# A late 4 MB zero fill sent as 120 rows on fifteen DMA engines and 8 rows on eight

## The chip, the cores and the metric

One core of a Trainium2 chip. The metric is the device time of one execution in microseconds (us). The four runs of the kernel before lie within 0.2% of each other (802.07 to 803.28); all runs compared here are of the fast state, except four kernels that ran once each and whose state is therefore unknown (marked "state unknown" below). Times in the profile count from the start of the span, that is from the first to the last instruction. The span of the kernel before is 802.6 us, its median time 802.9 us.

## The reference

A decoding step of attention over the last 4096 of 32768 cached positions, a gated feed-forward layer, and the gradients of all of it. What matters here is the gradient of the two caches: they have the caches' full shape, and outside the window they are zero.

```
"k_cache": (1, 8, 32768, 256)  bf16        # so is v_cache
W = min(4096, max(256, Sk // 4))           # 4096
k = jnp.repeat(k_cache[:, :, Sk - W:, :], rep, axis=1)
v = jnp.repeat(v_cache[:, :, Sk - W:, :], rep, axis=1)
...
_out, _vjp = jax.vjp(_f, A_x, A_k_cache, A_v_cache, ...)
_grads = _vjp(grad_out)
```

So 2 x 8 x 28672 x 256 zeros in bf16, 235 MB, have to be written, beside some 100 MB of loads and other results.

## The kernel before

SBUF is the core's on-chip memory; the fills read it as 128 partitions (rows, `p=128` below). Zeros lie in the arena in SBUF and are sent to the two outputs (`out_2`, `out_3`) in fills, large DMAs that write nothing but zeros. Most are issued on GpSimd's queue (`ZQ`), one after another until 700 us. The last ones, the late jobs, go out on SyncE's queue (`LD`), mixed with the last real results.

```
ZW = 8192
LD = nc.sync
ZQ = nc.gpsimd
... # cut
def zero_rows(o, g, n0, n1, f):
    reg = o[0, g, 0:Sk - W, :].rearrange("s d -> (s d)")[n0 * 128 * ZW:n1 * 128 * ZW]
    return reg.rearrange("(n p f) -> n p f", p=128, f=f)

late_jobs = [(out_2, G - 1, 5, 7, 2 * ZW), (out_3, G - 1, 0, 6, 2 * ZW), (out_3, G - 1, 6, 7, ZW)]
... # cut: everything else
            if it == 6:
                nc.vector.memset(ar(ZW, ZW), 0.0)

        for o, g, n0, n1, f in late_jobs:
            reg = zero_rows(o, g, n0, n1, f)
            for i in range(reg.shape[0]):
                LD.dma_start(out=reg[i], in_=ar(2 * ZW - f, f))
```

The late jobs are four fills of 128 rows of 32 KB (4 MB each) and one of 128 rows of 16 KB (2 MB). The last three DMAs of the program are called fill 2 (4 MB), fill 3 (4 MB, the one that is changed) and fill 4 (2 MB) below. The weight gradients' last rows are stored from 64 partitions.

```
LD.dma_start(out=ov[384:D, :], in_=buf[0:DQ, 3 * F:4 * F])      # 64 rows of 3584 bytes, twice
```

Of the kernel before, what the change touches and what calls it, by code (L numbers as in the profile page):

```python
# [26 lines left out]
ZW = 8192  # L27
# [6 lines left out]
def kernel(  # L34
# [3 lines left out]
    LD = nc.sync  # L38
# [14 lines left out]
    def ar(off, n):  # L53
        return arena[:, off:off + n]
# [59 lines left out]
# [3 lines that stand above are left out]
# [3 lines left out]
    for g in range(G):  # L120
        for o in (out_2, out_3):
            if g == G - 1 and o is out_3:
                continue
            reg = zero_rows(o, g, 0, 5 if g == G - 1 else NZ, ZW)
# [363 lines left out]
    with tc.tile_pool(name="work2", bufs=2) as work2, tc.tile_pool(name="lnw", bufs=1) as lnw, \  # L488
# [161 lines left out]
        for o, g, n0, n1, f in late_jobs:  # L650
            reg = zero_rows(o, g, n0, n1, f)
            for i in range(reg.shape[0]):
                LD.dma_start(out=reg[i], in_=ar(2 * ZW - f, f))

# [1 line left out]
_INS = ['A_x', 'A_k_cache', 'A_v_cache', 'A_wq', 'A_wo', 'B_x', 'B_w_gate', 'B_w_up', 'B_w_down', 'grad_out']  # L656
# [26 lines left out]
```

## Time and profile before

| | before |
|---|---|
| median time, before the experiments | 802.9 us (802.07 to 803.28, 4 runs) |
| span of the profiled run | 802.6 us |
| last compute instruction | about 720 us |
| bytes moved | 334.84 MB, 417 GB/s |
| last DMA packet ends | 801.1 us |

First the page of the kernel before. The first line is the busy time of each engine, the next two rows are the busy share of the sixteen DMA engines in tenths and the GB/s they moved, in forty equal slices of the span.

```profile
PE 460.6 (57%) x3157; PEld 247.8 (31%) x3180; DVE 368.5 (46%) x1173; ACT 196.1 (24%) x309; POOL 63.6 (8%) x112
DMA  9999999999999999999999999999999999999993
GB/s 354 430 430 431 429 428 430 429 429 429 428 424 425 425 419 403 420 423 426 428 421 412 429 430 429 427 428 427 426 425 425 425 425 424 422 408 423 429 438 171
DMA packets 29103, 334.84 MB, mean 417 GB/s; under 512 B 2819, under 2 KB 5638, under 8 KB 6918
...
out_dram<-arena SPq DMA_DIRECT2D x4, 4096.0 KB, 58.8
```

DMA is busy from end to end; the busiest compute engine, TensorE (PE), has 57%. So the kernel is done when the queues are drained, and the last slice, with 171 GB/s, says that the engines do not all finish together. Next the end of the kernel before by windows: for each stretch its length, the busy time of PE, PEld, DVE, ACT and POOL with the number of instructions, the granted clock of TensorE, the DMA engines' mean busy share and GB/s.

```profile
740.00:760.00 20.00, 0.00 (x0) 0.00 (x0) 0.00 (x0) 0.00 (x0) 0.00 (x0) 0.50 1.01 433
760.00:780.00 20.00, 0.00 (x0) 0.00 (x0) 0.00 (x0) 0.00 (x0) 0.00 (x0) 0.50 1.01 435
780.00:790.00 10.00, 0.00 (x0) 0.00 (x0) 0.00 (x0) 0.00 (x0) 0.00 (x0) 0.50 0.84 360
790.00:800.00 10.00, 0.00 (x0) 0.00 (x0) 0.00 (x0) 0.00 (x0) 0.00 (x0) 0.50 0.22 95
800.00:810.00 10.00, 0.00 (x0) 0.00 (x0) 0.00 (x0) 0.00 (x0) 0.00 (x0) 0.77 0.00 2
```

No compute at all, full rate until 780 us, then one engine after another runs dry. The trace also holds every DMA packet with its start, duration, size and queue, but not the number of the engine. An engine's next packet starts 3 or 4 ns before its last one ends, and the order of sizes in a queue is known from the program, so the packets (here one per row of a DMA) of the last 70 us can be strung to sixteen chains, one for each engine. They end at:

```
784.7 784.9 787.2 787.3 788.3 789.4 789.7 790.9 791.9 793.0 793.4 793.5 793.8 795.3 795.4 801.1
```

One engine is 5.7 us later than the next. It alone keeps the kernel from ending at 795.4. It is not that this engine moves its last packets more slowly: from fill 2 on, the packets of all sixteen chains take the same 1.21 us for 32 KB and 0.61 us for 16 KB.

The third view is again by windows, of the stretches in which the two 64-row stores move (708-716 and 720-728), and of those after them:

```profile
708.00:716.00 8.00, 3.54 (x18) 0.72 (x16) 5.18 (x10) 4.97 (x10) 0.00 (x0) 0.50 1.01 395
716.00:720.00 4.00, 1.23 (x8) 0.22 (x8) 2.59 (x5) 2.16 (x5) 0.00 (x0) 0.50 1.01 429
720.00:728.00 8.00, 0.00 (x0) 0.00 (x0) 0.56 (x1) 0.39 (x1) 0.00 (x0) 0.50 1.02 401
728.00:740.00 12.00, 0.00 (x0) 0.00 (x0) 0.00 (x0) 0.00 (x0) 0.00 (x0) 0.50 1.01 431
```

The engines are as busy as before (1.01, 1.02), yet move less. The prediction below counts the excess, about 10 us of packet time in each stretch.

### The profile page before, as it was taken

Reading aid. Unit: us, or ns where it says so; the run is one execution under the profiler, and the core shown is the slowest. Engines: PE = TensorE matmul, PEld = TensorE weight load, DVE = VectorE, ACT = ScalarE, POOL = GpSimd, SP = SyncE. Lnnn points to the kernel's source line nnn. Section 1 sums busy time; section 2 is a strip of 40 time slices with the busy share of each in tenths; the row PEclk is TensorE's granted clock in tenths of the full one; section 3 lists DMA queues with packets and bytes.
Section 4 is the critical chain, followed back from the end, with each engine's and each line's share of the span. In section 5 each row is a group of like instructions: output and inputs, shape, how many; then the busy total and the mean of one; then the engine's idle time right before and its main releaser. Section 6 shows DMA issues by size and latency. Waiting matters only on the chain.

```text
span 802.6 us, 8458 instructions
## 1 busy us (share of the span) xinstructions
PE 460.6 (57%) x3157; PEld 247.8 (31%) x3180; DVE 368.5 (46%) x1173; ACT 196.1 (24%) x309; POOL 63.6 (8%) x112
## 2 busy tenths in 40 slices
PE   0469999999999992622329397645263054630000
PEld 0334554545645551311219143322122012200000
DVE  2026264463462652255680876766691175860000
ACT  0143314223224000000002045543341034540000
POOL 4000000010100100011110010000000000000000
PEclk9989999999999997555559689776557557655555
DMA  9999999999999999999999999999999999999993
GB/s 354 430 430 431 429 428 430 429 429 429 428 424 425 425 419 403 420 423 426 428 421 412 429 430 429 427 428 427 426 425 425 425 425 424 422 408 423 429 438 171
DMA packets 29103, 334.84 MB, mean 417 GB/s; under 512 B 2819, under 2 KB 5638, under 8 KB 6918
## 3 DMA queue, kind: packets, MB, share of 16 engines
q0 software_dynamic: 17520, 216.01, 63.7%
q1 hardware_dynamic: 10102, 116.68, 34.7%
q10 hardware_dynamic: 1440, 1.61, 0.6%
q8 instruction: 25, 0.41, 0.2%
q14 instruction: 16, 0.13, 0.0%
HBM read 53.69 MB, written 280.59 MB: 416 GB/s over the span
## 4 chain that ended last, share of the span: by engine, by line
PE 35%; DMA 32%; DVE 16%; ACT 4%; issue 2%; another core or an unknown queue 0%; SPq 0%; ACTq 0%; DVEq 0%
DMA out_dram<-arena 17%; PE M_ps L311 10%; PE ok_ps L315 6%; PE rows_ps L255 6%; PE tr_ps L252 4%; DMA dh_bc<-in_grad_out_dram 4%; DMA arena<-in_A_k_cache_dram 4%; DMA arena<-in_A_wo_dram 3%; ACT arena L269 2%; DVE arena L640 2%; DVE arena L641 2%; DVE arena L452 2%; PE dqb_ps L495 2%; DMA arena<-in_B_w_up_dram 2%; DMA arena<-in_B_w_gate_dram 2%
## 5 line engine op out<-in xcount | busy, mean ns | idle before, releaser
L307 DVE TENSOR_SCALAR arena<-arena,p_f 128x256 bf16<-128x256 bf16 x512 | 109.9, 284 | 66.9 <-PE M_ps L311 35.7
L311 PE MATMUL M_ps<-arena 128*128 128x512 bf16 x489 | 120.1, 380 | 1.4 <-issue 0.2
L255 PE MATMUL rows_ps<-arena,vpad 128*16 128x512 bf16 x256 | 86.0, 430 | 23.3 <-DVE arena L603 16.8
L252 PE MATMUL tr_ps<-ident_bf,arena 128*128 128x128 bf16 x1024 | 88.5, 237 | 15.3 <-DMA arena<-in_A_k_cache_dram 9.5
L252 PEld LDWEIGHTS <-arena 128*128 128x128 bf16 x1024 | 66.3, 105 | 65.5 <-issue 54.9
L132 POOL DMA_DIRECT2D out_dram<-arena x82 | 45.1, 550 | 522.2 <-DMA out_dram<-arena 506.3
L269 ACT COPY arena<-tr_ps 128x1024 bf16<-128x1024 bf16 x64 | 61.8, 1015 | 88.6 <-PE tr_ps L252 88.6
L633 PE MATMUL d_ps<-arena,rT 32*128 32x512 bf16 x256 | 44.4, 507 | 63.1 <-DVE arena L641 37.6
L311 PEld LDWEIGHTS <-arena 128*128 128x128 bf16 x512 | 46.2, 99 | 50.8 <-issue 6.5
L315 PE MATMUL ok_ps<-arena 128*16 128x256 bf16 x512 | 57.5, 273 | 0.9 <-DVE arena L296 0.9
L601 ACT COPY arena<-tr_ps 128x1024 bf16<-128x1024 bf16 x32 | 32.5, 1016 | 97.7 <-PE tr_ps L252 40.4
L637 ACT CAST arena<-d_ps 128x512 bf16<-128x512 f32 x64 | 37.6, 587 | 69.5 <-PE d_ps L633 69.5
L640 DVE CAST arena<-d_ps 128x512 bf16<-128x512 f32 x64 | 44.0, 687 | 14.5 <-PE d_ps L633 14.3
L315 PEld LDWEIGHTS <-arena 128*16 128x16 bf16 x512 | 45.4, 90 | 13.9 <-issue 3.4
L641 DVE CAST arena<-d_ps 128x512 bf16<-128x512 f32 x64 | 43.6, 681 | 7.3 <-DMA out_dram<-arena 7.3
L638 ACT CAST arena<-d_ps 128x512 bf16<-128x512 f32 x64 | 38.1, 595 | 6.8 <-DMA out_dram<-arena 6.8
L633 PEld LDWEIGHTS <-rT 32*128 32x128 bf16 x256 | 11.2, 95 | 90.5 <-issue 58.2
L255 PEld LDWEIGHTS <-vpad 128*16 128x16 bf16 x256 | 19.1, 91 | 56.7 <-issue 49.1
L318 ACT COPY arena<-M_ps 128x512 f32<-128x512 f32 x16 | 8.6, 589 | 75.0 <-PE M_ps L311 75.0
L507 DVE CUSTOM_DVE_ANT_0 arena<-arena 128x4096 bf16<-128x4096 bf16 x3 | 13.1, 4423 | 24.3 <-ACT arena L500 24.3
L603 DVE COPY arena<-tr_ps 128x1024 bf16<-128x1024 bf16 x32 | 21.7, 682 | 3.7 <-PE tr_ps L252 3.7
L130 POOL DMA_DIRECT2D out_dram<-arena x21 | 14.0, 666 | 114.3 <-DMA out_dram<-arena 114.3
(196 smaller groups left out, 368.5 us busy)
## 6 DMA issues: line engine op xcount, KB each, us to landing
out_dram<-arena POOLq DMA_DIRECT2D x103, 2048.0 KB, 55.3
out_dram<-arena SPq DMA_DIRECT2D x18, 2048.0 KB, 33.3
arena<-in_A_v_cache_dram SPq DMA_DIRECT2D x10, 2048.0 KB, 49.9
arena<-in_A_k_cache_dram SPq DMA_DIRECT2D x8, 2048.0 KB, 29.4
out_dram<-arena SPq DMA_DIRECT2D x4, 4096.0 KB, 58.8
arena<-in_A_wq_dram SPq DMA_DIRECT2D x2, 3072.0 KB, 14.8
arena<-in_A_wo_dram SPq DMA_DIRECT2D x2, 1792.0 KB, 17.8
out_dram<-arena SPq DMA_DIRECT2D x2, 1792.0 KB, 32.6
```

Source lines behind the costliest of these rows:

```text
L132: ZQ.dma_start(out=reg, in_=zeros)
L252: nc.tensor.transpose(tr_ps[:, dh, i, :], X_sb[:, 4 * q + i, dh * 128:(dh + 1) * 128], ident_bf[:])
L255: nc.tensor.matmul(rows_ps[:], lhsT=pad[:, dh, 16 * q:16 * q + 16], rhs=XT[:, dh].rearrange("p t k -> p (t k)"), start=(q == 0 and dh == 0 ...
L269: sT_ps = dots(kv_at(K_off[g]), KT_slot, vpad[g % 2], rows1, ps_c, "cols", lambda q, XT, ps: nc.scalar.copy(out=XT, in_=ps))
L307: nc.vector.tensor_scalar(out=pK[:, i, hh, :], in0=K_sb[:, t, :], scalar1=p_f[:, 8 * i + c, hh:hh + 1], scalar2=None, op0=ALU.mult)
L311: nc.tensor.matmul(M_ps[:, vh, :], lhsT=V_sb[:, t, vh * 128:(vh + 1) * 128], rhs=pK[:, i, :, :].rearrange("p h d -> p (h d)"), start=(t == ...
L315: nc.tensor.matmul(ok_ps[:, k, :], lhsT=ppad[g % 2][:, 8 * (t % 4) + t // 4, :], rhs=X_sb[:, t, :], start=(g == 0 and k == 0 and t == 0), ...
L633: nc.tensor.matmul(d_ps[:, qi].rearrange("p w d -> p (w d)"), lhsT=rT[32 * q:32 * (q + 1), :], rhs=RB_[32 * q:32 * (q + 1), l, :], start=T ...
L637: nc.scalar.copy(out=stV[:, t:t + 2, :], in_=d_ps[:, :, 0, :])
L638: nc.scalar.copy(out=stK[:, t:t + 2, :], in_=d_ps[:, :, 1, :])
L640: nc.vector.tensor_copy(out=stV[:, t:t + 2, :], in_=d_ps[:, :, 0, :])
L641: nc.vector.tensor_copy(out=stK[:, t:t + 2, :], in_=d_ps[:, :, 1, :])
```

## The change

The intent: one DMA engine ends late, so take work from it. Of 128 rows over sixteen engines each has eight, as the chains show. Cut into 120 rows and 8 rows, the 120 are meant to use fifteen engines and not the late one, the 8 to use eight. Any partition will do as the source, since all hold zeros; the 8 rows are taken from partitions 0, 16, ..., 112.

```diff
         for o, g, n0, n1, f in late_jobs:
             reg = zero_rows(o, g, n0, n1, f)
             for i in range(reg.shape[0]):
-                LD.dma_start(out=reg[i], in_=ar(2 * ZW - f, f))
+                src = ar(2 * ZW - f, f)
+                if (n0, i) == (0, 2):
+                    LD.dma_start(out=reg[i, 0:120], in_=src[0:120])
+                    LD.dma_start(out=reg[i, 120:128], in_=src[0:128:16])
+                else:
+                    LD.dma_start(out=reg[i], in_=src)
```

No instruction moves on PE, VectorE, ScalarE or GpSimd, and SyncE issues one DMA more.

## The prediction

The forecast's sum came to this: if nothing slows, the end moves from 801.1 to 796.6 us, a gain of 4 us, which gives about 800 (one chance in four); if engines slow each other, 803 + 8.5 = 811.5 (three in four). Weighted, that is 808.6; the author said 810. "Such a case" in the third paragraph is one of engines that slow each other. Number 15 is the name for the engine that gets none of the 120 rows.

> **What bounds the kernel.** DMA. In the page's row of forty slices the DMA engines are 90% busy or more in all but the last, at about 425 to 430 GB/s; 334.84 MB move in 802.6 us. Compute ends at about 720 us (the table by windows), and what is left is queued zero fills, so only the drain of the DMA queues counts. The windows show 435 GB/s in 760-780, 360 in 780-790 and 74 in 790-803: the sixteen engines do not finish together. Following the packet records (a packet begins where the previous one on its engine ended) gives sixteen ends: 784.7 to 795.4 us for fifteen, 801.1 us for one, which moves its last seven 16 KB packets (0.61 us each) while all others idle. The mean is about 790.5: perfect balance would be worth some 10 us.
>
> **What the change does.** A 4 MB fill (128 rows of 32 KB, a packet of 1.21 us each, eight per engine) becomes 120 rows and 8 rows. No byte is added. [...] I take the late one for 15; the trace does not number engines. If nothing else changed, the end would be the next engine's, 795.4 + 1.2 = 796.6 instead of 801.1: a gain of 4 us. The extra issue on SyncE (0.3 to 1.8 us) lies at 729 us, some 50 us before its data moves: off the path.
>
> **What I expect to go wrong.** [...] The trace of before has such a case: the two 64-row stores of the weight gradients (3584 B rows, moving in 708-716 and 720-728 us). In just those stretches packets run long, in total 9.96 and 9.8 us of engine time over their undisturbed durations (0.61 us for 16 KB, 0.14 for 3584 B), against 0.2 and 0.5 in the stretches after them, and the rate falls from 430 to 395 and 401 GB/s. [...] Replaying the tail [...] the last engine ends 5 to 12 us later than before, 8.5 in the middle, even with engine 15 relieved.
>
> **Prediction.** Contention has three chances in four (about 811.5 us), none one in four (about 800). Predicted 810 us, range 799 to 817; faster by over 2%: 0.01, within 2%: 0.93, slower: 0.06.
>
> **What would show it.** Right: 32 KB packets of 1.8 to 2.4 us in the last 30 us (none now), a rate under 400 GB/s in slices that now have 430, a last end after 804 us. Wrong: all 32 KB packets stay at 1.21 us and the last engine ends near 797 us. One engine should show eight 32 KB packets fewer.
>
> **What would make it wrong.** [...] the late engine may not be number 15, so that its load isn't cut; stagger may keep the pairs apart.

## The result, and the profile after

| | before | after |
|---|---|---|
| median time | 802.9 us (4 runs) | 815.86 us (815.38 to 817.57, 4 runs) |
| ratio | | 1.0167 (1.0149 to 1.0184) |
| span of the profiled run | 802.6 us | 814.3 us |
| last DMA packet ends | 801.1 us | 812.9 us |
| packets of 32 KB over 1.4 us, of 512 | 1 | 92 |

A ratio is the mean time of one kernel's runs over that of the other's in the same rounds, so it is not quite the ratio of the medians. The change costs 13 us.

The same rows of the page after:

```profile
DMA  9999999999999999999999999999999999999993
GB/s 357 428 428 430 430 430 430 429 430 428 427 426 421 427 415 409 422 422 427 428 406 431 432 427 431 423 428 425 427 422 427 424 425 423 412 416 431 432 258 104
DMA packets 29111, 334.84 MB, mean 411 GB/s; under 512 B 2827, under 2 KB 5646, under 8 KB 6926
...
out_dram<-arena SPq DMA_DIRECT2D x3, 4096.0 KB, 59.6
...
out_dram<-arena SPq DMA_DIRECT2D x1, 3840.0 KB
```

The bytes are the same; all slices but the last two are within 20 GB/s of before. Those two hold 258 and 104 GB/s instead of 438 and 171. The windows after:

```profile
740.00:760.00 20.00, 0.00 (x0) 0.00 (x0) 0.00 (x0) 0.00 (x0) 0.00 (x0) 0.50 1.00 430
760.00:780.00 20.00, 0.00 (x0) 0.00 (x0) 0.00 (x0) 0.00 (x0) 0.00 (x0) 0.50 1.03 403
780.00:790.00 10.00, 0.00 (x0) 0.00 (x0) 0.00 (x0) 0.00 (x0) 0.00 (x0) 0.50 0.93 231
790.00:800.00 10.00, 0.00 (x0) 0.00 (x0) 0.00 (x0) 0.00 (x0) 0.00 (x0) 0.50 0.67 190
800.00:810.00 10.00, 0.00 (x0) 0.00 (x0) 0.00 (x0) 0.00 (x0) 0.00 (x0) 0.50 0.27 100
```

In 780-790 the engines are 93% busy and move 231 GB/s; before, 84% busy moved 360. The engines are not idle, their packets are slow. The timeline of SyncE's queue after (start, duration, line, operation):

```profile
722.53 1.84 SPq L658 DMA_DIRECT2D out_dram<-arena  x1
725.22 0.71 SPq L655 DMA_DIRECT2D out_dram<-arena  x1
728.80 0.64 SPq L656 DMA_DIRECT2D out_dram<-arena  x1
738.52 0.36 SPq L658 DMA_DIRECT2D out_dram<-arena  x1
```

All is issued by 739 us. Apart from one at 668 us, which before has too, the first slow 32 KB packet starts at 772.6, so the extra issue is off the path.

Strung to chains, the packets after show who did what. Exactly one chain has no packet of fill 3 (the prediction calls it 15), eight have the extra packet of the 8 rows, seven do not. Below are the durations of a chain's packets in fill 2, in the 120 rows and in the 8 rows, as multiples of 1.213 us, for the chain that ends last, for a typical one and for the one without fill 3; before, each of these numbers is 1.0.

```
ends    chain      fill 2 (8 packets)                 120 rows (8 packets)               8 rows
812.9   of eight   1.0 1.0 1.5 2.1 2.0 2.0 1.5 1.1    1.7 2.1 2.1 2.1 1.8 1.9 1.0 1.3    1.0
805.2   of eight   1.0 1.0 1.0 1.0 1.0 1.0 1.0 1.0    1.7 2.0 2.0 1.6 1.9 2.0 2.0 1.6    1.0
775.4   the one    1.0 1.0 1.0 1.0 1.0 1.0 1.0 1.0    none                               none
```

Twice the time, in runs of about four packets. Why four is not shown: the trace gives no partition of a packet. Note also fill 2 of the last chain: it is an untouched 128-row DMA, yet it is slowed. That fits other engines, already in their 120 rows, that slow it; the run with partitions 9 apart below shows such a case more clearly. Summed over all chains from 735 us on, packets of 16 and 32 KB took 137 us of engine time over their undisturbed durations; before, 3.5. Over sixteen engines the difference is 8.4 us each.

The last row is a surprise. The chain without fill 3 ended first of all, at 775.4. With the 8 x 1.21 = 9.7 us that were taken from it, it would have ended at 785.1: that is within 0.4 us of where the two earliest chains of before end, and 16 us from the late one.

### The profile page after: what moved, and what is told of

Read it like the earlier page. It is cut to its first block, busy times and chain, and to the rows that moved or that the text cites. A ratio compares the mean times of both kernels' runs of the same rounds, so it can differ in the third digit from the quotient of the medians.

```text
span 814.3 us, 8482 instructions
## 1 busy us (share of the span) xinstructions
PE 463.8 (57%) x3180; PEld 248.2 (30%) x3180; DVE 368.4 (45%) x1173; ACT 196.2 (24%) x309; POOL 62.7 (8%) x112
## 4 chain that ended last, share of the span: by engine, by line
DMA 45%; another core or an unknown queue 15%; DVE 14%; PE 9%; issue 3%; POOL 1%; ACT 1%; SPq 0%; DVEq 0%; ACTq 0%; POOLq 0%
DMA out_dram<-arena 45%; DVE arena L640 2%; DVE arena L641 2%; DVE arena L452 2%; PE dqb_ps L495 2%; PE rows_ps L255 2%; DVE arena L533 1%; PE d_ps L633 1%; DVE arena L626 1%; PE tr_ps L252 1%; POOL out_dram L132 1%; DVE arena L507 1%; DVE arena L423 1%; PE dqb_ps L498 1%
## 5 line engine op out<-in xcount | busy, mean ns | idle before, releaser
L311 PE MATMUL M_ps<-arena 128*128 128x512 bf16 x512 | 123.2, 382 | 0.0
```

Source lines behind the costliest of these rows:

```text
L311: nc.tensor.matmul(M_ps[:, vh, :], lhsT=V_sb[:, t, vh * 128:(vh + 1) * 128], rhs=pK[:, i, :, :].rearrange("p h d -> p (h d)"), start=(t == ...
```

## The experiments

The theory: engines whose source partitions go together slow each other when they read at the same time, and share what one gets undisturbed (32 KB in 1.213 us, which is 27.0 GB/s); the 120 rows bring such engines together. Below, that is called a collision. Which partitions go together the author assumed when choosing them; no run shows it as such. What the runs show is what each choice of source partitions cost. The rivals: fifteen engines, or a row count that is no power of two, are slow in themselves; or the 8 rows from partitions 16 apart do the harm. Where an expectation gives several times, the one that is not put down to a rival is the theory's. Apart from that: is the late engine the one that was relieved? "A replay" below is a small calculation of the last three fills with sixteen engines that start as staggered as in a measured trace; those that meet, by assumption, share evenly. Its figures are estimates.

Diffs are against the kernel before if not said otherwise. `reg[i]` is fill 3 under `(n0, i) == (0, 2)` and `src = ar(2 * ZW - f, f)`. All kernels gave correct results.

### Who is late: marks on the engines, before

Five small DMAs of k rows are cut out of fill 4 and placed between the fills. In the marked traces (table below) a mark of k rows is one packet on each of k chains, and the chains of a smaller mark are among those of every larger one. So the chains can be named by their marks: 0 has all of them, 1 to 3 have the 4-row mark but not the 1-row one, and so on to 12 to 15, which have none. The numbers mean no more than that.

```diff
+def tag(r0, k):
+    LD.dma_start(out=last[r0:r0 + k, 7680:ZW], in_=ar(ZW + 7680, 512)[0:k])
+# ahead of fill 2: tag(31, 1), tag(0, 12); ahead of fill 3: tag(12, 8); ahead of fill 4: tag(20, 7); at the end: tag(27, 4)
-LD.dma_start(out=reg[i], in_=src)                                   # fill 4
+LD.dma_start(out=last[:, 0:7680], in_=src[:, 0:7680])
+LD.dma_start(out=last[32:128, 7680:ZW], in_=src[32:128, 7680:ZW])
```

> The kernel before, with five small DMAs of 1, 12, 8, 7 and 4 rows of 1 KB cut out of the last fill, so that the packet records tell which engine numbers a chain belongs to [...]. Time: within 2 us of before (803). The prediction took the late engine for number 15: then the chain that ends last, some 5.7 us after the next, carries none of the marks. Rival, from the trace of after, where the chain without the third 4 MB fill ends first of all, at 775.4 us, which is 784.7 of before less its eight packets of 1.21 us: number 15 is the earliest engine, the late one carries the mark of the 8-row DMA, and if it is number 7[...] it has the 8-row and 12-row marks but not the 7-row one.

Measured (one run, state unknown): 803.33 us beside 803.43 for before. The chains by their marks:

```
engine 0        793.9
engines 1-3     792.3 792.7 796.4
engines 4-6     793.8 794.1 799.9
engine 7        792.5
engines 8-11    784.2 788.6 789.3 791.1
engines 12-15   785.0 788.6 789.0 789.3
```

Neither 15 nor 7 by these names: the late engine is one of 4 to 6, and the upper eight engines all end ahead of the lower eight. The prediction's premise is refuted, and so is number 7; the other half of the rival, that the late engine carries the 8-row mark, holds. The counts of packets fit: 1, 3, 3, 1, 4 and 4 chains carry the combinations of the table.

A second kernel with marks of 6 and 5 rows in place of 7 and 4 narrows it down.

> The kernel before with marks of 1, 12, 8, 6 and 5 rows. The first marked run put the late engine among numbers 4 to 6 (marks of 12, 8 and 7 rows, not of 4). Here it shows the 5-row and 6-row marks if it is number 4, only the 6-row mark if it is 5, neither if it is 6. A replay of the tail [...] ends the changed kernel at 812 us of the span for a late engine 4, 807 for 5 and 815 for 6; 812.9 was measured, so 4 or 6. If the lateness is random from run to run, another number comes out. Time 803.

Measured (one run, state unknown, another chip): 803.34 us. The last chain, at 799.8, carries the 5-row mark, so it is in 0 to 4; the next ends at 796.4. If one engine is late on both chips, and the marks name alike on both, it is number 4. Engines 12 to 15 end at 785.0 to 790.2 again.

### The same marks in the changed kernel

> The changed kernel with the same five marks. Time within 3 us of after (816). [...] Rival (fifteen engines are slow in themselves, or the writes to HBM are): all engines of the 120-row DMA are slow in the same way from its first packet on, whoever else is active. The late engine is the same as in the marked kernel before.

Measured (one run, state unknown): 816.38 us. The last chain ends at 813.0 and is again in 4 to 6; engine 7 ends at 802.8, the chain without fill 3 first, at 783.7 (here fill 4 was issued late for it, so this end is not the 775.4 of after). Slow packets come in runs of about four near 2.0 to 2.1, and the chains differ: engine 0 lost 0.7 us in its 32 KB packets, one of engines 12 to 14 lost 12.6. So it is not all engines in the same way. That each single slow packet has a partner that is slow at the same time was not checked in this run, since the marks give groups and not every number.

### One DMA on sixteen engines, source partitions 8 apart

```diff
-LD.dma_start(out=reg[i], in_=src)
+LD.dma_start(out=reg[i].rearrange("(e r) f -> e r f", r=8), in_=src[0:128:8].unsqueeze(1).to_broadcast([16, 8, f]))
```

Each block of eight rows comes from one partition: 0, 8, ..., 120.

> The third 4 MB fill again as one DMA of 128 rows on all sixteen engines[...]. Bytes, engines and destinations as before. [...] as slow as after or slower, 814 us (810 to 820), 32 KB packets of about 2.4 us. Rivals (fifteen engines, an uneven count, the separate 8-row DMA): 803 us, all 32 KB packets at 1.21 us.

Measured: 821.34 us (820.68 to 822.44, 4 runs), ratio 1.0219 (1.0201 to 1.0237). One DMA, 128 rows, all sixteen engines, no 8-row DMA, and it is slower than the change: 114 of 512 packets over 1.4 us. The rivals expected 803. The windows of this kernel, same columns:

```profile
760.00:780.00 20.00, 0.00 (x0) 0.00 (x0) 0.00 (x0) 0.00 (x0) 0.00 (x0) 0.50 1.05 384
780.00:790.00 10.00, 0.00 (x0) 0.00 (x0) 0.00 (x0) 0.00 (x0) 0.00 (x0) 0.50 0.98 187
790.00:800.00 10.00, 0.00 (x0) 0.00 (x0) 0.00 (x0) 0.00 (x0) 0.00 (x0) 0.50 0.82 202
```

98% busy at 187 GB/s: under half the rate for ten microseconds on end. The size was missed, 821 against at most 820 expected and 814 in the middle. The packets hint at more than pairs: of the 114, 58 took 2.1 times, nine 4.1 to 4.2 and only three 2.9 to 3.0. The replay shares evenly; where more than two engines slow each other that may be too kind. This was not tested by itself and is not shown.

### The eight rows from partitions 4 apart

Against the changed kernel:

```diff
-LD.dma_start(out=reg[i, 120:128], in_=src[0:128:16])
+LD.dma_start(out=reg[i, 120:128], in_=src[0:32:4])
```

> The changed kernel, but the 8 rows come from partitions 4 apart[...]. If the 120 rows are the cause: 815 us (813 to 818), as after. If the 8 rows from partitions 16 apart [...] are: 804.

Measured: 815.1 us (814.35 to 815.52, 4 runs), ratio 1.0149 (1.0134 to 1.0164), where the change has 1.0167. The last packet is at 812.0, where the change has 812.9. By the ratios the 8 rows' partitions are worth some 1.4 us, but the intervals overlap, so it may be nothing. The 120 rows are the cause.

### Fifteen engines, source partitions 9 apart

```diff
-LD.dma_start(out=reg[i], in_=src)
+LD.dma_start(out=reg[i, 0:120].rearrange("(e r) f -> e r f", r=8), in_=src[0:127:9].unsqueeze(1).to_broadcast([15, 8, f]))
+LD.dma_start(out=reg[i, 120:128], in_=src[0:32:4])
```

Each block of eight of the 120 rows comes from one partition: 0, 9, ..., 126. The author expected few collisions.

> The change's 120 and 8 rows on the same engines[...] and the 8 rows come from partitions 4 apart[...]. [...] faster than after by 5 to 11 us, about 809 us (805 to 812), with fewer packets over 1.4 us. Rival of fifteen engines: 816, as after. Rival of the 8 rows alone: 804.

Measured: 814.01 us (812.77 to 815.41, 4 runs), ratio 1.0128 (1.0111 to 1.0146): a miss by 2 us of the range's edge. Yet the windows say that most of the slowing is gone:

```profile
760.00:780.00 20.00, 0.00 (x0) 0.00 (x0) 0.00 (x0) 0.00 (x0) 0.00 (x0) 0.50 1.01 410
780.00:790.00 10.00, 0.00 (x0) 0.00 (x0) 0.00 (x0) 0.00 (x0) 0.00 (x0) 0.50 0.88 336
790.00:800.00 10.00, 0.00 (x0) 0.00 (x0) 0.00 (x0) 0.00 (x0) 0.00 (x0) 0.50 0.35 136
```

The loss over all chains is 42 us, not 137, and fifteen chains are done by 801.7. But the last one ends at 809.6: in fill 2 six of its packets took 2.0 to 2.1 times. That fits an engine already in its 120 rows that slows the late one. The chains show the partner: the last chain is slow from 776.6 to 794.7 us, and one other, the one that ends at 801.7, is slow from 777.4 to 795.6, in its 120 rows. Two more pairs of chains are slow together in this way (769.8 to 779.9 with 770.0 to 779.7, and 786.0 to 792.8 with 787.0 to 792.9). So the sum of the losses is not what the time follows; what the late engine meets is.

### Fifteen engines, source partitions 0 to 14

```diff
-LD.dma_start(out=reg[i], in_=src)
+LD.dma_start(out=reg[i, 0:120].rearrange("(e r) f -> e r f", r=8), in_=src[0:15:1].unsqueeze(1).to_broadcast([15, 8, f]))
+LD.dma_start(out=reg[i, 120:128], in_=src[0:32:4])
```

Each block of eight of the 120 rows comes from one partition, and the fifteen lie side by side.

> 120 rows on fifteen engines[...]. [...] the last engine ends near 830 us of the span, time 832 (826 to 840), 32 KB packets of about 4.9 us (four times 1.21). Rival, fifteen engines slow in themselves whatever partitions they read: 816.

Measured (one run, state unknown): 833.33 us beside 803.06, last packet at 830.1. The commonest slow packet took 4.2 times 1.213 us, as expected. The windows show the rate:

```profile
780.00:790.00 10.00, 0.00 (x0) 0.00 (x0) 0.00 (x0) 0.00 (x0) 0.00 (x0) 0.50 0.91 115
790.00:800.00 10.00, 0.00 (x0) 0.00 (x0) 0.00 (x0) 0.00 (x0) 0.00 (x0) 0.50 0.98 108
800.00:810.00 10.00, 0.00 (x0) 0.00 (x0) 0.00 (x0) 0.00 (x0) 0.00 (x0) 0.50 0.88 108
```

108 GB/s, by fifteen engines, are four times the 27.0 of one engine undisturbed. As many engines and the same rows, only other source partitions, cost 17 us more than the change, in the one run that there is: the number of engines is not it.

### Fifteen engines, source partitions 4 apart

The fifteen partitions are 32, 36, ..., 88, those of the 8 rows 0, 4, ..., 28. The author took this for a choice without collisions; that no 32 KB packet of the tail was slow in this run agrees.

```diff
-LD.dma_start(out=reg[i], in_=src)
+LD.dma_start(out=reg[i, 0:120].rearrange("(e r) f -> e r f", r=8), in_=src[32:89:4].unsqueeze(1).to_broadcast([15, 8, f]))
+LD.dma_start(out=reg[i, 120:128], in_=src[0:32:4])
```

> The change with every collision taken out: the 120 rows on fifteen engines[...]. If [...] engine 4 is the late one (the marks): all 32 KB packets at 1.21 us, and the end is engine 4's, one packet later than before: 804.3 us (803.5 to 805), no gain from relieving engine 15. If number 15 were the late engine, as the prediction took it: 799. If fifteen engines cost something in themselves: 810 or more.

Measured: 804.9 us (803.5 to 805.7, 5 runs), ratio 1.0023 (1.001 to 1.0037). In the tail every 32 KB packet is back at 1.0, the loss over all chains is 2.4 us, and the windows are those of before:

```profile
760.00:780.00 20.00, 0.00 (x0) 0.00 (x0) 0.00 (x0) 0.00 (x0) 0.00 (x0) 0.50 1.00 430
780.00:790.00 10.00, 0.00 (x0) 0.00 (x0) 0.00 (x0) 0.00 (x0) 0.00 (x0) 0.50 0.83 359
790.00:800.00 10.00, 0.00 (x0) 0.00 (x0) 0.00 (x0) 0.00 (x0) 0.00 (x0) 0.50 0.23 98
```

This is the change with its cost taken out and its intent left in. Rows, destinations and the number of engines are those of the change, and only the source partitions differ: so the cost lay on the reading side, not in fifteen engines and not in the writes. (That one partition is read again and again is not what helped: the runs with partitions 8 apart, 9 apart and 0 to 14 did the same and were slow.) And the intent gains nothing: the chain without fill 3 ends at 775.0, the late engine has one packet more, and the time is 0.2% above before.

### Taking work from the lower eight engines

The marks say that the upper eight end 9 to 16 us before the late one (the expectation's 4 is an error). This version is meant to give them fill 4, by GpSimd's queue.

```diff
-LD.dma_start(out=reg[i], in_=src)                                   # fill 4
+dst = reg[i].rearrange("(e r) f -> e r f", r=16)
+z8 = zeros[64:93:4].unsqueeze(1)
+ZQ.dma_start(out=dst[:, :, 0:512], in_=z8[:, :, 0:512].to_broadcast([8, 16, 512]))
+ZQ.dma_start(out=dst[:, :, 512:ZW], in_=z8[:, :, 512:ZW].to_broadcast([8, 16, ZW - 512]))
```

"If so" in the expectation is: if the fill falls on engines 8 to 15.

> Not the change, but what the marked run points to: in the kernel before, engines 8 to 15 end 4 to 15 us before the late one (784 to 791 against 799.9). The last 2 MB fill, 128 KB on each of sixteen engines, goes out on GpSimd's queue from eight partitions 64 to 92, 4 apart, behind a small DMA of eight partitions[...]. If so, engines 0 to 7 end 4.85 us earlier, 8 to 15 as much later: 798 us (797 to 800). If it lands on 0 to 7 instead, those end 4.85 us later [...]: 808 or more.

Measured: 799.39 us (798.42 to 800.72, 4 runs), ratio 0.995 (0.9934 to 0.9967). The last chain ends at 796.9 and has none of the moved packets; the eight that have them end at about 790 to 795.5 (two chains could not be told apart for part of the way). It is the fastest version here, half a per cent below before. The chain that ends last is probably the late engine's still, since without fill 4's 8 x 0.61 = 4.9 us that one would end at 796.3. Eight engines without the one that ends last were hit; why these is not shown. No marks show their numbers in this run.

A step further moves 512 KB of fill 3 as well, meant for engines 0 to 3:

```diff
 # the previous version, and:
-LD.dma_start(out=reg[i], in_=src)                                   # fill 3
+LD.dma_start(out=reg[i][:, 0:14336], in_=src[:, 0:14336])
+LD.dma_start(out=reg[i].rearrange("(e r) f -> e r f", r=32)[:, :, 14336:f], in_=src[0:16:4, 14336:f].unsqueeze(1).to_broadcast([4, 32, f - 14336]))
```

> The previous rebalancing (the last 2 MB fill on eight other engines by GpSimd's queue, 799.39 us, engine 4 last at 796.9 of the span, the eight at 790 to 795.5, the other seven of engines 0 to 7 at 788 to 790.5), and besides 512 KB of the third 4 MB fill moved from all sixteen engines to engines 0 to 3 ([...] 4 KB pieces): those end about 3.6 us later, all others 1.2 us earlier. Expected 798.2 us (797.3 to 799.2), the fastest of all; if the 4 KB pieces or GpSimd's queue cost something that I do not see, 800 or more.

Measured: 799.8 us (798.82 to 801.35, 5 runs), ratio 0.9964 (0.9951 to 0.9976): a miss, no better than the version before it. The last packets, until 796.7, are now the 4 KB ones, so an engine that got the moved part ends last; that it is one of 0 to 3 no mark shows. The first marked run had shown one of engines 1 to 3 at 796.4, which this expectation left out; that this is the reason is likely, but not shown.

## Why the prediction was right or wrong

- **DMA bounds the kernel, only the drain counts**: right. All slices but the last two are nearly as before, and the time moved with the last packet (801.1 to 812.9 us; spans 802.6 to 814.3).
- **The extra issue is off the path**: right. All was issued by 739 us.
- **"I take the late one for 15"**: wrong. In both marked runs of the kernel before, engines 12 to 15 end at 785 to 790 us and the late one is in the lower eight, by two runs number 4. So the 8 x 1.21 = 9.7 us that one engine loses are true (the chain without fill 3) and worth nothing, and in place of the gain of 4 us for the case without contention there is a small loss: 804.9 us was measured with no slow 32 KB packet left in the tail, where this branch had about 800.
- **Engines slow each other by where they read**: right. It is shown from three sides: slow packets without the change's fifteen engines (partitions 8 apart: 114 over 1.4 us, 821.3 us), fifteen engines without slow packets in the tail (4 apart, 804.9), and slower packets on as many engines (0 to 14: 4.2 times 1.213 us, 833.3). Which partitions go together, and which rows fall to which engine, is not shown.
- **The inference from the 64-row stores**: the long packets are there (9.96 and 9.8 us, 395 and 401 GB/s), and slowed packets came after the change too; that the two have one cause was the author's estimate and was not tested by itself.
- **The size**: 810 was said and 815.86 measured, in the range of 799 to 817. The contention branch had 8.5 us in the middle and 5 to 12; in the profile it is 11.8. The mis-sized term is what the last engine meets: the replay had put the late engine at number 15, where the load is cut. With engine 4 late, the replay ends at 812 us (807 for engine 5, 815 for 6), where 812.9 was measured; this one came after the result. For the partitions 0 to 14 it gave about 830 beforehand, where 830.1 was measured, but for those 8 apart 814 was expected and 821.3 measured. These are estimates, on assumptions that no run shows. The one-in-four for no contention drew the point further down. That the measured time still fell in the range is in part luck, since the range had to make up for the wrong late engine. The table below shows the term itself.
- **Eight engines get one packet more, 1.2 us each**: right, the trace after has eight such chains, and it falls on the late engine. With the partitions 4 apart, this and all else that is left of the change cost 2.2 us between medians (0.1% to 0.37%). What the 8 rows' source partitions add, which the prediction did not cost, is about 1 us or nothing.
- **The signs**: 32 KB packets of 1.8 to 2.4 us came, and a last end after 804. The rate under 400 GB/s came only from 780 us on (231); in 760-780 it was 403. One chain has eight 32 KB packets fewer, as said.

What the last chain of each run met, in us (loss is the time of its eight packets over 8 x 1.213):

| run | last packet ends | later than before | loss in fill 2 | loss in fill 3 | extra packet |
|---|---|---|---|---|---|
| the change | 812.9 | 11.8 | 5.1 | 7.4 | 1.2 |
| eight rows from partitions 4 apart | 812.0 | 10.8 | 10.4 | 0.3 | 1.2 |
| fifteen partitions, 9 apart | 809.6 | 8.5 | 8.1 | 0.5 | 1.2 |
| sixteen partitions, 8 apart | 818.6 | 17.5 | 16.6 | 0.0 | none |
| fifteen partitions, 4 apart | 801.7 | 0.5 | 0.0 | 0.0 | 1.2 |

In every row the three losses add up to the delay within 2 us, and the late engine's end by itself differs by 1.3 us between three traces without the change. In three of the four slow runs the last engine lost its time in fill 2, which nobody had touched.

Open: why engine 4 is late in the first place. It is late by about the same in all three traces of the kernel before and its marked forms (801.1, 799.9, 799.8), but what puts it behind in the 700 us before is not known. Strung back to 724 us, as far as the links are unique, the chains of before all have 1.44 to 1.47 MB left from SyncE's queue; from GpSimd's queue the late one has 0.62 MB left, the others 0.20 to 0.44. So it is behind in fills issued earlier. Whether it was slower, or had more to do (the 25 instruction fetches of queue 8 alone take 23 us of some engine or engines), was not tested. Also open is which partitions go together, and how engines share where three or more meet.

## What to carry to other kernels

When DMA bounds a kernel, ask which engine ends last before you take work from one: string the packets to chains, and mark engines with DMAs of k rows (here the marks fell on 1, 4, 7, 8 and 12 chains, each set within the next). Here 120 rows in place of 128 changed not only how many engines the DMA used (fifteen for sixteen); many of its packets took about twice as long, and it slowed the DMA around it too (fill 2 of the last chain, up to 2.1 times); ask this of any other row count. If the source may lie anywhere, as for zeros, try other source partitions: the same 120 and 8 rows took 815.86 us, 814.01 with partitions 9 apart and 804.9 with those 4 apart, where every 32 KB packet of the tail was back at 1.0. What counted here is not the sum of the losses (137 us in the change, 42 with partitions 9 apart, for 815.86 and 814.01 us) but what the last engine meets.
